# Holding the expert part of an attention and mixture-of-experts kernel to its source order

## The chip, the cores and the metric

The kernel runs on one NeuronCore of a Trainium2 chip. The metric is the device time of one execution in microseconds; for each kernel the median of its runs is given. TensorE (PE in the profile), VectorE (DVE), ScalarE (ACT), GpSimd (POOL) and SyncE (SP) each take their own list of instructions and wait for each other by semaphores.

## The reference, cut to what matters

```python
# block-sparse attention: batch 4, 8 heads, 768 positions, width 64
scores = q @ k.T / 8                      # masked by blocks of 32
attn = softmax(where(mask, scores, -1e9))
x = (attn @ v) laid out as 3072 tokens x 512
# experts: 8, hidden width 1024
P = balance(exp(x @ w_gate))              # 8 rounds of row and column scaling
for e in range(8):
    out += P[:, e:e+1] * (maximum(x @ w1[e], 0) @ w2[e])
```

## The kernel before, in words

The attention part comes first. Its work is put into numbered time slots by hand (the table `plan_at`), and the loop at L888 to L890 issues it slot by slot. `in_order` (L878) ties each instruction that a step issues to the newest one on the same engine, so that every engine takes the attention part's instructions in the order in which the loop issues them. The tie is a dependency without a semaphore, `behind` (L873).

The expert part follows in the source. It is cut into 32 iterations `i`: expert `e = i // 4` on a quarter of the tokens `b = i % 4`. Each iteration has two stages.

`stage1(i, qi)` (L1126), one of four quarters of the first matrix product, is a Strassen-like scheme: seven products `p0, p1, p5, p6, p3, p4, p2` in this order, each of six matmuls of 384 columns (L1135), since every operand is split into a high and a low 16-bit part and three of the four combinations are taken, for two halves of the inner dimension. A product's high weights feed the first two matmuls and the low weights the third. VectorE combines the products as they come (`comb`, L1145) into `r11`, `a1`, `u3`, `c21`; ScalarE copies the first product out of PSUM (L1180), applies the relu (L1184, L1200, L1204, L1212) and writes the high part of each result `h` (L1155); the low part is made by VectorE (L1159, L1165) or by GpSimd (L1165). GpSimd also forms four sums of the results (L1207, L1033). Four PSUM buffers `ph` hold products, so the fifth product of a row needs the first one's buffer back.

`stage2(i, p)` (L1233) takes the seven products of the second matrix, each in three pieces of twelve matmuls of 256 columns (L1248), and VectorE adds each piece into the output accumulator (L1269). Four other PSUM buffers, `py`, hold the pieces. In the main loop the pieces of iteration `i` stand between the quarters of iteration `i + 1`: p0, p1, quarter 0, p5, quarter 1, p6, p3, quarter 2, p4, p2, quarter 3.

Beside this regular work there is work per expert: the loads of `w1` and `w2` (L173, through one staging tile `r`), eight reductions for the scale of each (L187), the sums of weight quadrants on GpSimd (L1026) and the splits of the seven weight pieces into a high part on ScalarE (L1011) and a low part on VectorE (L1015). The first products of the next expert are in the last iteration of this one (`b == 3`): there, `w1` is split into the single buffers `arena` and `attic` that hold the seven pieces.

Which of this is written where is decided by the class `Slots` (L940). It counts ticks, one for each product or piece; it charges costs to three engines and issues queued work when it is due and fits. `need` (L993) issues what a coming product requires at once, just ahead of that product (L1131, L1236 to L1240). The order in which the source issues is thus a plan. But the program is built with `schedule_with_timeline_sim=True` (L1385), and in the expert part nothing ties the instructions to that plan: the scheduler lines each engine's instructions up by its own simulation, under the true dependencies alone. It also moves instructions of the expert part in among the last of the attention part, and the attention's leftovers (`finish_x`, L348) ahead of where the source has them. `PIN` is 0, so `InOrder` (L893) passes calls through.

Of the kernel before, what the change touches and what calls it, by code (L numbers as in the profile page):

```python
# [55 lines left out]
def tile_sparse_attention_moe(  # L56
# [11 lines left out]
    nc = tc.nc  # L68
# [156 lines left out]
    def load_x1(i, p):  # L225
        nc.sync.dma_start(out=xp[p], in_=xd[i % B][:, p])
# [168 lines left out]
    with ExitStack() as actx:  # L395
# [479 lines left out]
        )  # L875
        newest = {}

        def in_order(fn, *a):  # L878
            n = len(nc.cur_bb.bb.instructions)
            fn(*a)  # L880
            for ins in nc.cur_bb.bb.instructions[n:]:
                if ins.engine in newest:
                    tc.add_manual_dep(
                        ins, newest[ins.engine], behind, reason="keep_in_program_order"
                    )
                newest[ins.engine] = ins.name

        for T in range(min(plan_at), max(plan_at) + 1):  # L888
            for _, _, fn, a in sorted(plan_at.get(T, ()), key=lambda x: x[:2]):
                in_order(fn, *a)  # L890
        xlast = finish_x(B - 1)

    class InOrder:  # L893
        def __init__(self, engine):
# [226 lines left out]
    def load_x(i):  # L1121
        b = i % B
        for p in PORDER:
            load_x1(i, p)
# [183 lines left out]
    for i in range(NI):  # L1308
# [48 lines left out]
        quarter(3)  # L1357
        if i + 2 < NI:
            load_x(i + 2)

# [27 lines left out]
```

## Time and profile before

| | before |
|---|---|
| median of 3 runs | 2358.24 us (2353.56 to 2359.13) |
| profiled execution, own time | 2357.4 us |
| its span | 2355.6 us |
| mean granted TensorE clock | 0.986 |
| busy: PE, DVE, ACT, POOL | 2200.1, 2014.4, 1256.0, 1287.1 us |

The page of the profile gives for each engine the time in which it worked and, for each group of instructions, the idle time ahead of them and who ended it. The chain of waits follows the last instruction back to what released it. The view by windows gives the busy time of every engine in chosen stretches, with the granted clock of TensorE; the view in order of time gives single instructions, with start and duration, where instructions alike that follow each other are one row. Time in rows is counted from the start of the span. An iteration's place is found by counting the matmuls of L1135 and L1248.

### The profile page before, as it was taken

How to read it: one execution, taken by the hardware profiler on the slowest of the kernel's cores; microseconds unless marked ns; L12 is line 12 of the kernel's file. 1: busy time of each engine (PE TensorE's matmuls, PEld its weight loads, DVE VectorE, ACT ScalarE, POOL GpSimd, SP SyncE). 2: the span in 40 equal slices, each digit the busy share in tenths (PEclk: the TensorE clock that was granted, in tenths of full speed). 3: DMA queues.
4: the chain of work that ended last, by engine and by line, in shares of the span. 5: the costliest groups of instructions: out<-in, count | busy, mean ns of one | idle time of the engine just before them, and what ended most of it. 6: DMA issues, size and time to landing. Idle time of an engine off the chain costs nothing.

```text
span 2355.6 us, 47334 instructions
## 1 busy us (share of the span) xinstructions
PE 2200.1 (93%) x18892; PEld 1608.6 (68%) x18892; DVE 2014.4 (86%) x3570; ACT 1256.0 (53%) x2173; POOL 1287.1 (55%) x1235
## 2 busy tenths in 40 slices
PE   5999998879999999999989999999899999998999
PEld 3766666647666677677667776776677667766777
DVE  8999999888789878987898789878987898789876
ACT  4888878655465445444444445444544454445442
POOL 2012334496367645765576557655865486548543
PEclk9999999999999999999999999999999999999999
DMA  6667765422121212121212121212211221121221
GB/s 152 135 123 151 186 131 121 135 97 75 48 82 50 83 48 83 48 83 48 83 48 83 48 84 52 80 48 83 64 68 48 84 80 52 48 84 48 75 75 54
DMA packets 191888, 192.34 MB, mean 82 GB/s; under 512 B 131740, under 2 KB 144052, under 8 KB 191668
## 3 DMA queue, kind: packets, MB, share of 16 engines
q1 hardware_dynamic: 191104, 189.30, 28.2%
q8 instruction: 147, 2.41, 0.4%
q14 instruction: 73, 0.60, 0.1%
q10 hardware_dynamic: 564, 0.03, 0.0%
HBM read 140.54 MB, written 17.30 MB: 67 GB/s over the span
## 4 chain that ended last, share of the span: by engine, by line
PE 57%; DVE 21%; POOL 9%; issue 6%; DMA 4%; ACT 3%; SPq 0%; DVEq 0%; POOLq 0%; ACTq 0%
PE py L1248 25%; PE p L1135 23%; POOL r L1026 3%; DVE top L673 3%; DMA r<-in_moe_w_dram 3%; DVE h L1165 2%; PE u L731 2%; POOL h L1165 2%; DVE u L1145 2%; DVE acc L1269 2%; DVE mx_w L187 2%; PE t L697 1%; PE m L664 1%; PE t L700 1%; PE m L667 1%
## 5 line engine op out<-in xcount | busy, mean ns | idle before, releaser
L1248 PE MATMUL py<-w2p,h 128*128 128x256 f16 x8064 | 971.1, 275 | 52.7 <-ACT h L1155 23.7
L1248 PEld LDWEIGHTS <-h 128*128 128x128 f16 x8064 | 790.1, 99 | 209.9 <-ACT h L1155 28.8
L1269 DVE SCALAR_TENSOR_TENSOR acc<-py,spare,acc 128x256 f32<-128x256 f32 (+1 forms) x840 | 459.2, 581 | 49.5 <-PE py L1248 46.9
L1165 POOL TENSOR_TENSOR h<-u,h 128x384 f16<-128x384 f32 x128 | 127.0, 992 | 601.3 <-ACT h L1155 601.3
L1135 PEld LDWEIGHTS <-attic 128*128 128x128 f16 x3072 | 301.8, 98 | 195.9 <-issue 22.5
L1135 PE MATMUL p<-attic 128*128 128x384 f16 x2304 | 413.2, 328 | 16.4 <-DVE r L1145 14.4
L1135 PE MATMUL p<-arena 128*128 128x384 f16 x2304 | 407.6, 327 | 19.4 <-DVE a L1145 11.2
L1135 PEld LDWEIGHTS <-arena 128*128 128x128 f16 x2304 | 225.9, 98 | 153.5 <-issue 24.8
L1155 ACT ACTIVATE h<-c 128x384 f16<-128x384 f32 x256 | 133.6, 522 | 330.7 <-DVE c L1145 256.7
L705 ACT ACTIVATE pe<-t,shift,qk 128x768 int32<-128x768 f32 x192 | 189.7, 989 | 78.6 <-PE t L700 73.0
L1145 DVE SCALAR_TENSOR_TENSOR a<-p,a 128x384 f32<-128x384 f32 x384 | 211.1, 550 | 18.9 <-PE p L1135 14.3
L673 DVE TENSOR_REDUCE top<-m 128x1 f32<-128x768 f32 x192 | 181.8, 949 | 16.7 <-PE m L667 16.4
L1155 ACT ACTIVATE h<-r 128x384 f16<-128x384 f32 x256 | 132.5, 521 | 66.5 <-POOL r L1033 63.0
L1207 POOL TENSOR_TENSOR s<-a,u 128x384 f32<-128x384 f32 x128 | 129.6, 1013 | 68.7 <-ACT a L1204 68.7
L1033 POOL TENSOR_TENSOR r<-s,r 128x384 f32<-128x384 f32 x128 | 155.4, 1214 | 9.6
L1033 POOL TENSOR_TENSOR c<-c,r 128x384 f32<-128x384 f32 x128 | 150.8, 1178 | 10.0
L1135 PE MATMUL p<-arena,attic 128*128 128x384 f16 x768 | 146.1, 327 | 0.0
L1026 POOL TENSOR_TENSOR r<-r 128x256 f32<-128x256 f32 (+1 forms) x106 | 135.0, 1290 | 20.0 <-DVE arena L1015 17.9
L664 PE MATMUL m<-kt,qt 128*128 128x512 f16 (+1 forms) x384 | 129.6, 338 | 14.5 <-DVE top L673 7.2
L1165 POOL TENSOR_TENSOR h<-r,h 128x384 f16<-128x384 f32 x128 | 142.8, 1115 | 0.2 <-ACT h L1155 0.2
L1145 DVE SCALAR_TENSOR_TENSOR r<-p,a 128x384 f32<-128x384 f32 x128 | 70.7, 552 | 79.0 <-PE p L1135 59.4
L697 PE MATMUL t<-qt,kt 128*128 128x512 f16 (+1 forms) x384 | 127.9, 333 | 10.8 <-DVE top L673 10.6
(206 smaller groups left out, 3683.1 us busy)
## 6 DMA issues: line engine op xcount, KB each, us to landing
arena<-xd SPq DMA_DIRECT2D x128, 384.0 KB, 3.9
attic<-xd SPq DMA_DIRECT2D x96, 384.0 KB, 3.9
r<-in_moe_w_dram SPq DMA_DIRECT2D x16, 2048.0 KB, 8.4
arena<-in_q_dram SPq DMA_DIRECT2D x16, 384.0 KB, 4.5
arena<-in_k_dram SPq DMA_DIRECT2D x16, 384.0 KB, 4.8
arena<-in_v_dram SPq DMA_DIRECT2D x4, 1536.0 KB, 8.5
xd<-xs_t SPq DMA_DIRECT2D x16, 384.0 KB, 4.6
out_dram<-acc SPq DMA_DIRECT2D x24, 256.0 KB, 2.0
```

Source lines behind the costliest of these rows:

```text
L664: nc.tensor.matmul(sc[:, lo:hi], lhsT=qt[:, 0, c], rhs=ka[:, lo:hi], start=True, stop=False)
L673: nc.vector.tensor_reduce(out=tops[n][:, c : c + 1], in_=sc[:, :S], axis=AX.X, op=ALU.max)
L697: nc.tensor.matmul(sc[:, lo:hi], lhsT=kt[:, 0, c], rhs=qa[:, lo:hi], start=True, stop=False)
L705: nc.scalar.activation(pe, sc[:, :S], AF.Exp, bias=shift, scale=qk[n // 2][3])
L1026: lambda c=c: Pinned.gpsimd.tensor_tensor(out=out[:, c], in0=x[:, c], in1=y[:, c], op=op),
L1033: nc.gpsimd.tensor_tensor(out=out, in0=x, in1=y, op=ALU.subtract)
L1135: nc.tensor.matmul(ps, lhsT=w1p[p][:, l, kc, fs], rhs=xp[p][:, r, kc], start=(kc == 0 and m == 0), stop=(kc == KH - 1 and m == 2),)
L1145: nc.vector.scalar_tensor_tensor(out=t, in0=ps, scalar=HDOWN, in1=other, op0=ALU.mult, op1=ALU.add)
L1155: nc.scalar.activation(h[:, 0], src, AF.Relu if relu else AF.Copy)
L1165: eng.tensor_tensor(out=h[:, 1], in0=src, in1=h[:, 0], op=ALU.subtract)
L1248: nc.tensor.matmul(py, lhsT=hs[i, p, kc][:, l, tsl], rhs=w2p[p][:, r, kc], start=(kc == 0 and m == 0), stop=(kc == KF // 2 - 1 and m == 2),)
L1269: nc.vector.scalar_tensor_tensor(out=dst, in0=src, scalar=c, in1=dst, op0=ALU.mult, op1=ALU.add)
```

## The change

The list of traced instructions is kept, the tie is put into a function of its own, `hold_from(n)`, and the length of the list at the end of the attention part is remembered. At the end of the kernel every instruction issued since then is tied to the newest before it on its engine. No instruction is added or taken away, no operand or size differs. Lines after L890 stand six further down.

```diff
+        traced = nc.cur_bb.bb.instructions
+
+        def hold_from(n):
+            for ins in traced[n:]:
                 if ins.engine in newest:
                     tc.add_manual_dep(
                         ins, newest[ins.engine], behind, reason="keep_in_program_order"
                     )
                 newest[ins.engine] = ins.name
 
+        def in_order(fn, *a):
+            n = len(traced)
+            fn(*a)
+            hold_from(n)
+
         for T in range(min(plan_at), max(plan_at) + 1):
...
         xlast = finish_x(B - 1)
+        held = len(traced)
...
         if i + 2 < NI:
             load_x(i + 2)
+    hold_from(held)
```

What this does to the engines' lists is shown at three places. In the names, `p5_12_0` is product p5 of iteration 12, quarter 0, and the last number of a name only tells tiles apart.

**VectorE where the first products of expert 3 begin** (iteration 12, quarter 0, with stage 2 of iteration 11 around it). L1015 (after: L1021) are the low parts of the `w1` splits: a split that reads `s3` is that of product 6. Before:

```order
L1015 SCALAR_TENSOR_TENSOR attic_96<-s3_3_14764,sw1_3_14762,attic_96 128x1024
L1145 SCALAR_TENSOR_TENSOR u3_11_3_16024<-p6_11_3_16025,a1_11_3_15995 128x384
L1165 TENSOR_TENSOR h_5_8094<-r11_11_3_16004,h_5_8094 128x384
L1015 SCALAR_TENSOR_TENSOR attic_96<-r1_3_14758,sw1_3_14762,attic_96 128x1024
L1145 SCALAR_TENSOR_TENSOR c21_11_3_16033<-p3_11_3_16034,u3_11_3_16024 128x384
L1015 SCALAR_TENSOR_TENSOR arena_92<-r1_3_14758,sw1_3_14762,arena_92 128x1024
L1015 SCALAR_TENSOR_TENSOR attic_96<-r1_3_14758,sw1_3_14762,attic_96 128x1024
L1145 SCALAR_TENSOR_TENSOR u3_11_3_16024<-p4_11_3_16044,u3_11_3_16024 128x384
L1145 SCALAR_TENSOR_TENSOR a1_11_3_15995<-p4_11_3_16044,a1_11_3_15995 128x384
L1015 SCALAR_TENSOR_TENSOR attic_96<-r1_3_14758,sw1_3_14762,attic_96 128x1024
```

Now:

```order
L1021 SCALAR_TENSOR_TENSOR arena_92<-r1_3_14758,sw1_3_14762,arena_92 128x1024
L1151 SCALAR_TENSOR_TENSOR r11_12_0_16193<-p1_12_0_16194,a1_12_0_16184 128x384
L1171 TENSOR_TENSOR h_0_8089<-r11_12_0_16193,h_0_8089 128x384
L1151 SCALAR_TENSOR_TENSOR a1_12_0_16184<-p5_12_0_16205,a1_12_0_16184 128x384
L1021 SCALAR_TENSOR_TENSOR attic_96<-s3_3_14764,sw1_3_14762,attic_96 128x1024
L1151 SCALAR_TENSOR_TENSOR u3_12_0_16215<-p6_12_0_16216,a1_12_0_16184 128x384
L1021 SCALAR_TENSOR_TENSOR attic_96<-r1_3_14758,sw1_3_14762,attic_96 128x1024
L1151 SCALAR_TENSOR_TENSOR c21_12_0_16224<-p3_12_0_16226,u3_12_0_16215 128x384
L1021 SCALAR_TENSOR_TENSOR attic_96<-r1_3_14758,sw1_3_14762,attic_96 128x1024
L1151 SCALAR_TENSOR_TENSOR u3_12_0_16215<-p4_12_0_16237,u3_12_0_16215 128x384
L1151 SCALAR_TENSOR_TENSOR a1_12_0_16184<-p4_12_0_16237,a1_12_0_16184 128x384
L1021 SCALAR_TENSOR_TENSOR attic_96<-r1_3_14758,sw1_3_14762,attic_96 128x1024
```

The splits stood among the combinations of the last quarter of iteration 11; now those of products 6, 3, 4 and 2 stand one by one between the combinations of iteration 12's first quarter, each behind the combination of the product just ahead of it.

**ScalarE where iteration 13 begins.** `w2p_5` and so on are the high parts of the `w2` splits, `a1_13_0` the copy of the first product out of PSUM, `h` from `s1`, `a1`, `r11`, `c21` the high parts of the sums that GpSimd makes. Before:

```order
L1155 ACTIVATE h_23_8112<-u3_12_3_16734 128x384
L1212 ACTIVATE c21_12_3_16744<-c21_12_3_16744 128x384
L1204 ACTIVATE a1_12_3_16700<-a1_12_3_16700 128x384
L1011 ACTIVATE w2p_5_8087<-t2_3_16273,sw2_3_16271 128x1024
L1011 ACTIVATE w2p_6_8088<-r2_3_16267,sw2_3_16271 128x1024
L1180 ACTIVATE a1_13_0_16894<-p0_13_0_16895 128x384
L1011 ACTIVATE w2p_3_8085<-r2_3_16267,sw2_3_16271 128x1024
```

Now:

```order
L1161 ACTIVATE h_24_8113<-s1_12_3_16778 128x384
L1161 ACTIVATE h_25_8114<-a1_12_3_16700 128x384
L1161 ACTIVATE h_26_8115<-r11_12_3_16710 128x384
L1161 ACTIVATE h_27_8116<-c21_12_3_16744 128x384
L1017 ACTIVATE w2p_5_8087<-t2_3_16273,sw2_3_16271 128x1024
L1017 ACTIVATE w2p_6_8088<-r2_3_16267,sw2_3_16271 128x1024
L1017 ACTIVATE w2p_3_8085<-r2_3_16267,sw2_3_16271 128x1024
L1017 ACTIVATE w2p_4_8086<-r2_3_16267,sw2_3_16271 128x1024
L1186 ACTIVATE a1_13_0_16894<-p0_13_0_16895 128x384
```

The copy stood behind two splits; now four high parts that wait for GpSimd and four splits stand ahead of it.

**SyncE's loads around the first loads for expert 4.** `xd` are the stored tokens of a quarter, `r1` and `r2` the weights. Before:

```order
L173 DMA r2_3_16267<-in_moe_w2_dram 128x8x512
L226 DMA arena_92<-xd_1_77 128x1536 x4
L226 DMA attic_96<-xd_1_77 128x1536 x3
L173 DMA r1_4_17448<-in_moe_w1_dram 128x4x1024
L226 DMA arena_92<-xd_2_78 128x1536 x4
L226 DMA attic_96<-xd_2_78 128x1536 x3
```

Now:

```order
L173 DMA r2_3_16267<-in_moe_w2_dram 128x8x512
L226 DMA arena_92<-xd_1_77 128x1536 x4
L226 DMA attic_96<-xd_1_77 128x1536 x3
L226 DMA arena_92<-xd_2_78 128x1536 x4
L226 DMA attic_96<-xd_2_78 128x1536 x3
L173 DMA r1_4_17448<-in_moe_w1_dram 128x4x1024
```

The load of the next `w1` now stands behind seven token loads, the last of which waits for the end of iteration 13's first stage.

4 lines of the change are left out of this document (removed).

## The prediction

> **What bounds the kernel now.** I read the page first, then the chain of waits, the windows and single instructions in order of time. The page:
>
> ```profile
> span 2355.6 us, 47334 instructions
> PE 2200.1 (93%) x18892; PEld 1608.6 (68%) x18892; DVE 2014.4 (86%) x3570; ACT 1256.0 (53%) x2173; POOL 1287.1 (55%) x1235
> PE 57%; DVE 21%; POOL 9%; issue 6%; DMA 4%; ACT 3%; SPq 0%; DVEq 0%; POOLq 0%; ACTq 0%
> ```
>
> TensorE is the largest share of the chain. The chain in order of time gives its pace and the rhythm of the experts:
>
> ```profile
> 805.34 3.90 PE p L1135 x24
> 812.71 7.32 PE py L1248 x67
> ...
> 931.79 8.52 DMA r<-in_moe_w_dram
> ...
> 2101.10 8.50 DMA r<-in_moe_w_dram
> ```
>
> A matmul of stage 1 takes 3.90/24 = 0.1625 us, one of stage 2 7.32/67 = 0.109 us. An expert has 672 of the one and 1008 of the other: 109.2 + 110.1 = 219.3 us. The same load recurs after five experts: (2101.10 - 931.79)/5 = 233.9 us. So TensorE loses 14.6 us per expert. Three windows show where: the last iteration of one expert (11), the first of the next (12), and an ordinary one (columns: busy time of PE, weight loads, DVE, ACT, POOL, each with its count, granted clock, DMA).
>
> ```profile
> 1152.00:1214.00 62.00, 57.18 (x431) 41.57 (x429) 57.96 (x99) 31.63 (x57) 35.22 (x31) 1.00 0.27 86
> 1214.00:1270.00 56.00, 50.27 (x371) 36.23 (x369) 52.17 (x81) 25.36 (x48) 46.61 (x44) 0.97 0.23 78
> 1277.00:1328.00 51.00, 51.00 (x397) 38.78 (x396) 40.74 (x78) 23.59 (x47) 27.02 (x28) 1.00 0.14 48
> ```
>
> Ordinary iterations have no idle TensorE at all; nothing can be gained there. All that an order can win back is the 14.6 us at seven expert changes, about 102 us, and the start. VectorE is nearly full at the change (57.96 of 62), so where it stands waiting there is what matters.
>
> **The change part by part.** No work is added. Each term is a wait that an ordered engine meets.
>
> Durations, from the groups by form and single instructions in order of time:
>
> ```profile
> L1207 POOL TENSOR_TENSOR s<-a,u 128x384 f32<-128x384 f32 x128 | 129.6, 1013 | 68.7 <-ACT a L1204 68.7
> L1033 POOL TENSOR_TENSOR r<-s,r 128x384 f32<-128x384 f32 x128 | 155.4, 1214 | 9.6
> L1165 POOL TENSOR_TENSOR h<-r,h 128x384 f16<-128x384 f32 x128 | 142.8, 1115 | 0.2 <-ACT h L1155 0.2
> L1026 POOL TENSOR_TENSOR r<-r 128x512 f32<-128x512 f32 x42 | 68.5, 1651 | 17.9 <-DVE arena L1015 17.9
> L1026 POOL TENSOR_TENSOR r<-r 128x256 f32<-128x256 f32 x64 | 66.5, 1053 | 2.2 <-DVE w2p L1015 2.2
> L1011 ACT ACTIVATE w2p<-r,sw 128x1024 f16<-128x1024 f32 x48 | 53.9, 1141 | 59.8 <-POOL r L1026 54.4 <-DVE sw L204 5.4
> ...
> L1180 ACT ACTIVATE a<-p 128x384 f32<-128x384 f32 x128 | 61.5, 481 | 57.5 <-PE p L1135 56.2 <-POOL s L1026 0.2
> ...
> L1015 DVE SCALAR_TENSOR_TENSOR w2p<-r,sw,w2p 128x1024 f16<-128x1024 f32 x48 | 78.3, 1634 | 12.0 <-ACT w2p L1011 12.0
> ```
> ```profile
> 1162.39 1.27 DVE L1015 SCALAR_TENSOR_TENSOR attic<-r,sw,attic 128x1024 f16<-128x1024 f32 x1
> 1290.34 0.56 DVE L1145 SCALAR_TENSOR_TENSOR r<-p,a 128x384 f32<-128x384 f32 x1 [1.54 <-PE p L1135]
> 1292.04 0.56 DVE L1165 TENSOR_TENSOR h<-r,h 128x384 f16<-128x384 f32 x1 [0.24 <-ACT h L1155]
> ```
> ```profile
> 1290.93 0.52 ACT L1184 ACTIVATE r<-r 128x384 f32<-128x384 f32 x1 [1.15 <-DVE r L1145]
> 1291.48 0.52 ACT L1155 ACTIVATE h<-r 128x384 f16<-128x384 f32 x1
> ```
>
> *First quarter of a new expert.* Zero is where stage 2 of iteration 11 starts. TensorE needs 72 x 0.109 = 7.9 us for p0 and p1, then seven products of 0.975 us: the quarter would end at 14.7. Product 5 needs a split of a quadrant that GpSimd subtracts after the first split has read it. GpSimd, in order, still has the previous quarter (its first low part, then s, a, r, c, five at 1.0 to 1.2, from about 1.8 to 7.2), then half a sum (1.65), two low parts (2.1), the other half (1.65): 12.6. ScalarE's high part takes it to 13.7, VectorE's low part to 15.0; the two first matmuls need only the high part, the other four and their drain take 0.8: product 5 is there at 15.8 instead of 10.8. From here the rows of VectorE above run one after the other. ScalarE copies product 0 behind the split of product 6 (13.7 + 1.14 + 0.48 = 15.3); `r11` starts, its low part 1.70 later (1292.04 - 1290.34), `a1` at 17.5, the split for product 6 until 19.2, product 6 at 20.0; then `u3` 0.55, the next split 1.2, product 0.8: 22.6; then `c21` 0.55, ScalarE's high part 0.52, its split 1.14, VectorE's 1.2, product 0.8: 26.9; then `u3`, the relu and high part of it, both splits, the last product: 0.5 + 1.1 + 1.14 + 1.2 + 0.7 = 4.7: 31.6. The quarter ends 16.9 us late. Before, the splits ran ahead, with the first product's stall of 1.66 us and one of 1.38 us the only ones around it:
>
> ```profile
> 1164.65 1.14 PE L1135 MATMUL p<-arena 128*128 128x384 f16 x6 [1.66 <-DVE a L1145]
> 1167.16 4.26 PE L1248 MATMUL py<-w2p,h 128*128 128x256 f16 x34 [1.38 <-DVE acc L1269]
> ```
>
> Bounds: 12 us, if half of the sums' part is already over when the stretch begins, to 19 with the splits at the 1.63 us that they average under GpSimd's traffic.
>
> *Start of the next iteration.* The 15 sums for `w2` that stand before GpSimd's part of the last quarter take 15 x 1.05 = 15.8 us, with two low parts 18; TensorE gives that part some 9.5 us to wait in, of which about 1.5 is spent: `s`, `a`, `r`, `c` come about 6.5 us late. ScalarE now waits for all four, then has four splits (4 x 1.14), and only then copies the first product: 7.2 + 6.5 + 4.6 = 18.3 us after the quarter's end, while TensorE fills its four PSUM buffers by 7.9 + 3.9 = 11.8. That is 6.5 us, and VectorE's queued splits and the scale of `w2` add some 4.5: I take 11. Before, the same trap shut once here, ScalarE waiting for GpSimd and TensorE for ScalarE:
>
> ```profile
> 1233.38 1.15 ACT L1011 ACTIVATE w2p<-r,sw 128x1024 f16<-128x1024 f32 x1 [3.72 <-POOL r L1026]
> ```
> ```profile
> 1237.93 3.53 PE L1248 MATMUL py<-w2p,h 128*128 128x256 f16 x17 [3.21 <-ACT h L1155]
> ```
> ```profile
> 1234.00:1242.00 8.00, 4.77 (x27) 2.86 (x26) 7.33 (x9) 3.34 (x7) 6.41 (x6) 0.79 0.53 183
> ```
>
> Bounds: 5.7 (the idle time of the second window above, 56 - 50.27) to 16.
>
> These rows also show a price behind a wait: 17 matmuls took 3.53 us where 17 x 0.109 = 1.9 would do, with a granted clock of 0.79. The stalls of the first quarter are shorter, and the 1.66 and 1.38 us above left the clock at 1.00. I put nothing for it in the sum, and 1.6 us for each change in the upper end. [...]
>
> *The load of w1.* It waited only for its staging tile before, was issued in iteration 12 and its maxima ran at once:
>
> ```profile
> 1236.49 0.38 SPq L173 DMA_DIRECT2D r<-in_moe_w_dram  x1
> ```
> ```profile
> 1175.17 1.87 DVE L187 TENSOR_REDUCE mx_w<-r 128x1 f32<-128x512 f32 x3 [2.27 <-DMA r<-in_moe_w_dram]
> 1247.67 4.82 DVE L187 TENSOR_REDUCE mx_w<-r 128x1 f32<-128x512 f32 x8
> ```
> ```profile
> 1165.81 0.38 SPq L173 DMA_DIRECT2D r<-in_moe_w_dram  x1
> ```
>
> Such a load took 1175.17 - 1165.81 = 9.4 us. Now it goes out about 1 us into iteration 13, behind the token loads, and lands at 10.4 or later; VectorE comes to the first maximum at 8.5 to 9 and stands there, the next quarter's combinations behind it. With two PSUM buffers of slack I take 3 us; bounds 0 and 5. In return the 4.82 us of maxima leave the crowded iteration 12; that is in the 11 above.
>
> A change of experts then costs 16.9 + 11 + 3 = 30.9 us instead of 14.6: 16.3 more, seven times, 114 us.
>
> *Ordinary quarters.* VectorE now waits for the low part of `r11` before the next combination (1.14 us idle, 1290.90 to 1292.04). A quarter behind six pieces absorbs it in its PSUM buffers. The quarter behind three pieces only (p5) finds the copy of its first product behind high part `r` on ScalarE: by the rows above its sixth buffer is about 0.3 us late. 31 times 0.35 is 11 us; bounds 0 and 30.
>
> *Start.* Before, stage 1 began at 462.2:
>
> ```profile
> L1135 PE MATMUL p<-arena x2304: 322/326/524, 462.2 to 2320.3; 128*128 128x384 f16 x192
> ...
> 462.00:560.00 98.00, 84.25 (x668) 58.02 (x666) 82.33 (x136) 54.45 (x105) 76.48 (x69) 0.96 0.16 59
> ```
>
> Now it begins behind the last transposes of the attention, which follow the normalisation of the last head and the scale of `w2`: about 468, 5.7 later. Four quarters then run without pieces between them, each bound by the loop TensorE, VectorE, ScalarE, GpSimd, and `finish_x` makes TensorE wait in the open; but before, the 98 us also held 13.75 idle. I take 12 us in all; bounds 0 and 25.
>
> The sum: 2357.4 + 114 + 11 + 12 = 2494 us. The profiled execution is 0.8 us under the median, which changes nothing: I say 2494.
>
> **The rivals.**
> 1. *The plan smooths the expert change.* For it: VectorE's 4.82 us of maxima and GpSimd's sums for `w1` leave the busiest iteration, and the plan spreads the rest by due times. If the splits were ready one product ahead, the idle time of the first window (62 - 57.18 = 4.8 us) would go and about a third of the second one's 5.7, 6.7 us at each change, and with the start unchanged that gives 2357.4 - 7 x 6.7 = 2310 us. It decides in the first quarter: below about 5 us lost there the change gains. Against it: the order puts four splits behind combinations that need the very product before, so they can't be ahead. Chance 0.06.
> 2. *Only the first quarter pays.* The stops let the others catch up, so that 16.9 replaces all of the 14.6 and nothing follows it: 2357.4 + 7 x 2.3 + 11 + 12 = 2396 us. For it: VectorE was full before, and a stop of TensorE frees it. Chance 0.14.
> 3. *The waits reach ordinary quarters.* For it: VectorE has 40.74 busy of 51 there, and two waits of about 1 us in each of four quarters take 8 of the 10 that are left. If a third of them comes through, 0.7 us a quarter, 31 x 4 x 0.7 = 87 us come on top: 2581 us. Against it: PSUM buffers carry it over. Chance 0.14.
> 4. *The order changes nothing that counts* (within 0.3%, about what a measurement of this kernel can tell from no change): 0.02. That the ties do not hold is ruled out by the engines' lists.
>
> **How the numbers follow.** My forecast has 0.64. Its own bounds are 7 x (12 + 5.7 + 0 - 14.6) = 22 and 7 x (19 + 16 + 5 + 1.6 - 14.6) = 189, with 0 to 55 for the rest; not all ends meet, so it goes from 2410 to 2580. The range of 2396 to 2585 takes in rivals 2 and 3 and leaves out 1 and the ends of the others. Slower: 0.64 + 0.14 + 0.14 = 0.92; same 0.02; faster 0.06.
>
> **What would show it.** Right: the first products of experts 1 to 7 stand four matmuls at a time, 2 to 4 us apart, with TensorE idle behind VectorE's splits; ScalarE stands before its first `w2` split of an iteration after an expert change and TensorE behind the copy; the load of experts recurs after about 250 us; ordinary windows stay full. Wrong: a period under 234 us, or idle time of TensorE in the windows of ordinary iterations of more than 1 us each.

## The result, and the profile after

The tied kernel takes 2606.55 us (median of 4 runs, 2603.8 to 2616.57) beside 2357.37 us of the kernel before: a ratio of 1.1067, 95% interval 1.1034 to 1.1101. The order costs 249 us; the prediction said 2494 us, 137 more than before, and at most 2585.

The profiled execution took 2616.57 us. Its first matmul of stage 1 came at 470.2 us; in the other profiled runs, whose attention part is the same, it lies anywhere from 456.5 to 470.4. So the stages are counted here from that matmul. The page, to set beside the three lines of before:

```profile
span 2614.6 us, 47460 instructions
...
PE 2284.1 (87%) x18892; PEld 1627.5 (62%) x18892; DVE 1998.0 (76%) x3570; ACT 1270.0 (49%) x2173; POOL 1248.8 (48%) x1235
...
PE 44%; DVE 27%; POOL 10%; ACT 8%; issue 7%; DMA 4%; SPq 0%; DVEq 0%; POOLq 0%
```

TensorE's share of the chain fell from 57 to 44%, VectorE's rose from 21 to 27%. And 18892 matmuls, the same as before, are busy for 2284.1 us instead of 2200.1: the same work takes 84 us more inside the matmuls. The windows show where (columns: busy time of PE, weight loads, DVE, ACT, POOL with counts, granted clock, DMA): the first quarter of expert 3; the first of the next iteration; the one in which `w1` lands; an ordinary iteration but for its last quarter; and the stretch with the four quarters of iteration 0, which begin at 470.2.

```profile
1272.90:1301.80 28.90, 13.48 (x45) 4.38 (x43) 15.43 (x19) 9.85 (x13) 9.48 (x8) 0.60 0.00 1
1355.00:1370.70 15.70, 9.72 (x44) 4.99 (x43) 12.17 (x16) 9.34 (x13) 7.21 (x7) 0.78 0.00 0
1420.50:1431.50 11.00, 8.21 (x45) 4.50 (x44) 7.94 (x16) 1.81 (x4) 1.78 (x2) 0.87 0.16 67
1474.70:1523.70 49.00, 48.26 (x380) 37.08 (x379) 37.03 (x68) 21.82 (x45) 26.88 (x27) 1.00 0.08 27
462.00:510.00 48.00, 38.07 (x242) 22.71 (x240) 29.85 (x54) 21.85 (x43) 22.59 (x23) 0.82 0.15 49
```

A quarter is 42 matmuls of 0.1625 us, 6.83 us at full pace. The first takes 28.9 us and no engine is busy for much more than half of it: they wait for each other. TensorE's instructions there in order of time, with the idle time ahead of each and who ended it:

```profile
1275.12 0.50 PE L1141 MATMUL p<-arena 128*128 128x384 f16 x2 [1.08 <-ACT arena L1017]
1277.09 0.82 PE L1141 MATMUL p<-arena 128*128 128x384 f16 x4 [1.47 <-DVE arena L1021]
1280.26 0.82 PE L1141 MATMUL p<-arena 128*128 128x384 f16 x2 [2.35 <-ACT arena L1017]
1282.61 1.46 PE L1141 MATMUL p<-arena 128*128 128x384 f16 x4 [1.53 <-DVE arena L1021]
...
1299.04 0.82 PE L1141 MATMUL p<-attic 128*128 128x384 f16 x2 [2.80 <-ACT attic L1017]
1300.36 1.46 PE L1141 MATMUL p<-attic 128*128 128x384 f16 x4 [0.50 <-DVE attic L1021]
1301.61 4.59 PE L1254 MATMUL py<-w2p,h 128*128 128x256 f16 x22
```

Two matmuls behind ScalarE's high part, four behind VectorE's low part, product after product: the predicted rhythm. Not predicted is that the same four matmuls take 0.82 us at 1277.09 and 1.46 at 1282.61, and 22 of stage 2 then 4.59 where 22 x 0.109 = 2.4 would do.

The other two foreseen places are there as well. ScalarE waits for GpSimd's sums ahead of splits of `w2`, copies the first product only behind them, and TensorE, with its four buffers full, waits for that copy:

```profile
1362.47 2.19 ACT L1017 ACTIVATE w2p<-r,sw 128x1024 f16<-128x1024 f32 x2 [1.12 <-POOL r L1032]
1364.57 0.47 ACT L1186 ACTIVATE a<-p 128x384 f32<-128x384 f32 x1
```
```profile
1365.09 5.78 PE L1141 MATMUL p<-attic 128*128 128x384 f16 x18 [5.98 <-ACT a L1186]
```

The load of `w1` is issued, takes 10.5 us to land, and VectorE's first maxima wait for it:

```profile
1413.27 0.38 SPq L173 DMA_DIRECT2D r<-in_moe_w_dram  x1
...
1423.73 3.06 DVE L187 TENSOR_REDUCE mx_w<-r 128x1 f32<-128x512 f32 x5 [1.92 <-DMA r<-in_moe_w_dram]
```

In iteration 0, TensorE waits for the first `w2` split, which ScalarE has behind the quarters, and for the attention's leftovers on VectorE:

```profile
519.82 0.37 PE L1254 MATMUL py<-w2p,h 128*128 128x256 f16 x1 [5.89 <-ACT w2p L1017]
577.96 0.19 PE L369 MATMUL lg<-gh,xs_b 128*128 128x8 f16 x1 [5.80 <-DVE xs_b L355]
```

Counting matmuls gives each iteration's length, from the end of its predecessor's stage 2 to the end of its own. Means over experts 1 to 6, in us; full pace is 219.3/4 = 54.8. "Start" runs from the first matmul of stage 1 to the end of stage 2 of iteration 2.

| kernel | b = 3 | b = 0 | b = 1 | b = 2 | sum | first quarter | start | over before, same chip |
|---|---|---|---|---|---|---|---|---|
| before | 60.2 | 64.0 | 54.9 | 54.8 | 233.9 | mixed | 218.3 | |
| all tied | 80.4 | 67.2 | 62.1 | 55.8 | 265.4 | 28.9 | 255.6 | 249.2 |
| e1 start only | 60.4 | 64.0 | 54.9 | 54.8 | 234.2 | mixed | 253.3 | 41.5 |
| e2 changes only | 80.0 | 67.2 | 62.0 | 55.9 | 265.0 | 28.9 | 226.0 | 214.3 |
| e3 filler | 77.5 | 67.2 | 62.0 | 55.8 | 262.5 | 26.9 | 255.2 | 234.6 |
| e4 early splits | 71.3 | 66.3 | 61.8 | 55.8 | 255.1 | 7.1 | 255.3 | 179.6 |
| e5 staggered | 71.9 | 66.1 | 61.8 | 55.8 | 255.6 | 8.8 | 255.2 | 181.7 |
| e6 late maxima | 80.0 | 67.2 | 59.9 | 55.8 | 263.0 | 28.9 | 253.1 | 235.1 |
| e7 costs | 77.8 | 74.8 | 61.9 | 55.8 | 270.3 | 28.9 | 259.8 | 293.6 |
| e9 TensorE only | 70.0 | 64.9 | 54.9 | 54.8 | 244.6 | 12.9 | 225.8 | 71.6 |
| e10 all but TensorE | 79.5 | 66.9 | 59.7 | 54.2 | 260.3 | 34.3 | 250.7 | 212.5 |
| e11 VectorE only | 70.1 | 66.5 | 57.0 | 53.8 | 247.5 | 28.0 | 273.6 | 144.0 |
| e12 all but VectorE | 80.4 | 63.6 | 60.6 | 54.9 | 259.5 | 26.0 | 224.2 | 178.8 |
| e13 VectorE, ScalarE free | 74.3 | 61.3 | 59.3 | 54.8 | 249.7 | 20.5 | 218.3 | 111.7 |
| e14 ScalarE only | 40.8 | 96.0 | 60.8 | 54.8 | 252.5 | 30.8 | 232.9 | 140.6 |

So 37 us of the 249 arise in the start (255.6 - 218.3), the rest behind it, nearly all at the expert changes and the loads of `w1`. "Mixed" means that pieces of stage 2 stand inside the quarter; that is so in e10, e11 and e14 too, so their quarters can't be set beside the others. The last column is the difference of the medians. Each experiment has two runs (e15 seven); the 95% interval of such a difference is 7 to 9 us either way, and 12 to 13 for e1 and e18.

### The profile page after: what moved, and what is told of

It reads as the page before. It is cut to its first block, busy times and chain, and to the rows that moved or that the text cites. A ratio compares the mean times of both kernels' runs of the same rounds, so it can differ in the third digit from the quotient of the medians.

```text
span 2614.6 us, 47460 instructions
## 1 busy us (share of the span) xinstructions
PE 2284.1 (87%) x18892; PEld 1627.5 (62%) x18892; DVE 1998.0 (76%) x3570; ACT 1270.0 (49%) x2173; POOL 1248.8 (48%) x1235
## 4 chain that ended last, share of the span: by engine, by line
PE 44%; DVE 27%; POOL 10%; ACT 8%; issue 7%; DMA 4%; SPq 0%; DVEq 0%; POOLq 0%
PE py L1254 19%; PE p L1141 17%; ACT h L1161 3%; DVE acc L1275 3%; DMA r<-in_moe_w_dram 3%; POOL r L1032 3%; DVE h L1171 3%; DVE top L673 3%; DVE u L1151 2%; POOL h L1171 2%; DVE a L1151 2%; DVE mx_w L187 2%; PE u L731 2%; POOL s L1213 1%; DVE attic L1021 1%
## 5 line engine op out<-in xcount | busy, mean ns | idle before, releaser
L1254 PE MATMUL py<-w2p,h 128*128 128x256 f16 x8064 | 923.9, 276 | 14.8 <-ACT w2p L1017 6.8
L1254 PEld LDWEIGHTS <-h 128*128 128x128 f16 x8064 | 799.5, 99 | 134.7 <-issue 14.8
L1141 PE MATMUL p<-attic 128*128 128x384 f16 x2304 | 456.6, 349 | 152.9 <-DVE a L1151 46.0
L1275 DVE SCALAR_TENSOR_TENSOR acc<-py,spare,acc 128x256 f32<-128x256 f32 (+1 forms) x840 | 449.6, 581 | 37.9 <-PE py L1254 26.6
L673 DVE TENSOR_REDUCE top<-m 128x1 f32<-128x768 f32 x192 | 181.9, 950 | 18.7 <-PE m L667 18.3
L1171 DVE TENSOR_TENSOR h<-r,h 128x384 f16<-128x384 f32 x128 | 89.4, 699 | 134.4 <-ACT h L1161 134.2
L1161 ACT ACTIVATE h<-r 128x384 f16<-128x384 f32 x256 | 133.9, 523 | 81.8 <-POOL r L1039 77.8
L1171 DVE TENSOR_TENSOR h<-s,h 128x384 f16<-128x384 f32 x128 | 111.1, 868 | 79.5 <-ACT h L1161 78.7
L1141 PE MATMUL p<-arena,attic 128*128 128x384 f16 x768 | 154.6, 338 | 12.1 <-DVE attic L1021 12.1
L1190 ACT ACTIVATE r<-r 128x384 f32<-128x384 f32 x128 | 66.9, 523 | 183.0 <-DVE r L1151 183.0
L1039 POOL TENSOR_TENSOR r<-s,r 128x384 f32<-128x384 f32 x128 | 145.8, 1139 | 10.0
L664 PE MATMUL m<-kt,qt 128*128 128x512 f16 (+1 forms) x384 | 130.0, 339 | 14.6 <-DVE top L673 7.2
L1206 ACT ACTIVATE u<-u 128x384 f32<-128x384 f32 x128 | 66.9, 523 | 150.1 <-DVE u L1151 148.0
```

Source lines behind the costliest of these rows:

```text
L664: nc.tensor.matmul(sc[:, lo:hi], lhsT=qt[:, 0, c], rhs=ka[:, lo:hi], start=True, stop=False)
L673: nc.vector.tensor_reduce(out=tops[n][:, c : c + 1], in_=sc[:, :S], axis=AX.X, op=ALU.max)
L1039: nc.gpsimd.tensor_tensor(out=out, in0=x, in1=y, op=ALU.subtract)
L1141: nc.tensor.matmul(ps, lhsT=w1p[p][:, l, kc, fs], rhs=xp[p][:, r, kc], start=(kc == 0 and m == 0), stop=(kc == KH - 1 and m == 2),)
L1161: nc.scalar.activation(h[:, 0], src, AF.Relu if relu else AF.Copy)
L1171: eng.tensor_tensor(out=h[:, 1], in0=src, in1=h[:, 0], op=ALU.subtract)
```

## The experiments

In what follows "over before" is the last column of the table, and each text in front of a result is what was expected of it. Theory at the outset: the predicted waits are the right ones, and TensorE's clock, which falls behind them (0.60 over the first quarter, in the windows above), makes them longer. Rivals: steady losses in ordinary quarters, the start, one engine's order alone, or plain lack of VectorE's time.

**Where it is lost.** In e1 the tie ends at iteration 2, as the diff shows, and in e8 at iteration 1; in e2 it begins at iteration 2 (`held = len(traced)` there); in e16 it holds for two of four iterations.

```diff
         if i == 2:
             finish_late()
+            hold_from(held)
...
-    hold_from(held)
```

> Only the instructions from the end of the attention part to the beginning of iteration 2 are tied; the rest is lined up by the scheduler as before. Theory (the traces put some 45 us of the 249 into the start and the rest into the seven expert changes): 2357 + 45 = 2402 us, 2385 to 2415. Rival (the start costs what the prediction gave it, 12 us, and the waits of the changes are spread wider than they look): 2369 us, 2360 to 2380.

It took 2397.65 us, 41.5 over before, as the theory had it. The prediction's 12 us is ruled out: the interval of the ratio begins at 1.0117, which is 28 us.

> Only the instructions from iteration 2 on are tied. Theory: 2357 + 7 x 30 = 2570 us, 2550 to 2590, with the same waits at the changes as in the changed kernel. Rival (the late start of the changed kernel puts its later order out of step and causes part of these waits): under 2530 us.

It took 2570.38 us, 214.3 over before, as the theory had it. Together, 41.5 + 214.3 = 255.8 us come near the 249 of the tied kernel: start and changes are nearly independent.

> Tied only from the end of the attention part to the beginning of iteration 1: the first iteration's quarters, the products of iteration 0 with the quarters of iteration 1 between them, not the balance rounds' second half and the attention's leftovers in iteration 1. Theory (about half of the start's 41 us is lost there, by quarters that run without pieces between them, the rest in iteration 1 by the leftovers and the balance): 2357 + 20 = 2377 us, 2368 to 2385. Rival (one of the halves holds it all): 2357 to 2362 us, or 2393 to 2400 us.

It took 2392.74 us, 34.1 over before, at the edge of what the rival said: tying no more than the first iteration costs most of the start's 41.5, and by their intervals the two can't be told apart. What the free scheduler wins back in iteration 1 it loses in the next, and by stage 2's end of iteration 2 the start is 245.6 long, beside 253.3 in e1 and 218.3 before. TensorE waits 11.64 us in the open for the attention's leftovers:

```profile
582.27 0.19 PE L369 MATMUL lg<-gh,xs_b 128*128 128x8 f16 x1 [11.64 <-DVE xs_b L355]
```

For e16, the iterations with b = 1 and 2 are tied one by one from expert 1 on (`if i > 2 and b in (1, 2): hold_from(held)`, `held` renewed in each).

> Tied are only the instructions that iterations b = 1 and b = 2 of each expert issue, the load of w1, its maxima and the ordinary quarters among them; the changes of experts proper and the start are free. Theory: the step of b = 1 rises from 54.9 to about 62 us, that of b = 2 from 54.8 to 55.8 us, eight experts at the most: 2358 + 55 to 65 = 2413 to 2423 us. Rival (the wait for w1 follows from the late iteration 12 of the tied order and goes without it): 2358 to 2385 us.

It took 2407.9 us, 50.8 over before: 5 us under the theory's range, but much nearer to it than to the rival's. The lengths of its iterations are 59.7 (b = 1) and 55.8 (b = 2), and the free ones beside them lose too (62.8 and 64.6). An ordinary iteration loses 1.0 us, the load of `w1` about 4.8; the rest of the 7.3 in the tied kernel must come with its surroundings, which are tied there too.

**The clock.** e3 gives TensorE something to do in the waits:

```diff
+            if i and i % B == 0 and qi == 0 and p in (6, 3, 4, 2):
+                for _ in range(9):
+                    nc.tensor.matmul(
+                        ps, lhsT=w1p[0][:, 0, 0, fs], rhs=xp[0][:, 0, 0],
+                        start=True, stop=True,
+                    )
             for kc in range(KH):
```

> The changed kernel with nine more matmuls of 384 columns ahead of products 6, 3, 4 and 2 of the first quarter of each new expert, on operands that are there already, into the product's own PSUM buffer, which the product then starts afresh: 4 x 9 x 0.1625 = 5.9 us of work for TensorE in waits of about 3.8 us each. Theory (the low clock behind waits is a cost of its own): the granted clock of that quarter rises from 0.60 to 0.8 or more, its groups of four matmuls take 0.65 to 0.9 us instead of 1.46, the 22 matmuls behind it 2.4 to 3.2 instead of 4.59, and seven changes gain 4 to 6 us each: 2565 to 2580 us. Rival (the four matmuls are slow for another reason, or the clock doesn't follow the busy share): 1.46 us as before and 2606 us or up to 40 us more.

It took 2590.71 us, 234.6 over before: 14.6 less than the tied kernel, a third to a half of what the theory gave. Its rows show the mechanism (single instructions, the first ahead of the filler, the others behind it; the page; the window of the quarter):

```profile
1270.38 1.46 PE L1147 MATMUL p<-arena 128*128 128x384 f16 x4 [1.53 <-DVE arena L1021]
...
1286.57 0.82 PE L1147 MATMUL p<-attic 128*128 128x384 f16 x4 [0.82 <-DVE attic L1021]
1287.23 4.09 PE L1260 MATMUL py<-w2p,h 128*128 128x256 f16 x36
```
```profile
PE 2292.7 (89%) x19144; PEld 1643.5 (64%) x19144; DVE 1998.7 (77%) x3570; ACT 1270.7 (49%) x2173; POOL 1248.6 (48%) x1235
```
```profile
1260.60:1287.30 26.70, 16.44 (x82) 7.63 (x80) 15.49 (x19) 9.86 (x13) 9.55 (x8) 0.87 0.00 1
```

With filler, four matmuls take 0.82 us again and 36 of stage 2 take 4.09, with the granted clock at 1.00 from 1287.30 to 1291.20; over the quarter it is 0.87 instead of 0.60. But the quarter is still 26.7 us long: the clock of this quarter is some 2 to 3 us of each change (14.6/7; 80.4 to 77.5), the chain of engines the rest. It may be a little more, since two of the four fillers had no wait left behind them and so stood in the way themselves.

**The splits of `w1`.** e4 issues the first four among the combinations of the quarter ahead of the change, the other three around stage 2's first products:

```diff
         comb(a1, product(5), a1)
+        if split:
+            split(0)
...
         if last:
-            split_w1(e + 1)
+            after[i](4)
         stage2(i, 0)
+        if last:
+            after[i](5)
         stage2(i, 1)
```

> The changed kernel, all tied, but the source issues the splits of w1 earlier: the first four among the combinations of the last quarter ahead of the change, the other three around stage 2's first two products. Theory (these splits between the combinations are what stretches the first quarter to 28.9 us): that quarter falls to 8 to 12 us, at full clock, VectorE's queue gives 2 to 4 us back in the quarter before, and seven changes gain 13 to 20 us each: 2470 to 2515 us. Rival (VectorE and GpSimd are full there, so the wait only moves into stage 2 or the quarter before): over 2560 us.

It took 2535.72 us, 179.6 over before: between the two. The quarter fell from 28.9 to 7.1 us, at a granted clock of 0.97. But the iteration fell from 80.4 to 71.3 only; over half of the gain went into waits earlier in it, in stage 2:

```profile
1248.08 0.40 PE L1279 MATMUL py<-w2p,h 128*128 128x256 f16 x1 [6.15 <-DVE h L1182]
1252.72 5.30 PE L1279 MATMUL py<-w2p,h 128*128 128x256 f16 x24 [4.25 <-DVE acc L1300]
```

e5 takes the waits out of that chain: each low part stands one product behind its high part, and product 6 is split ahead of product 5. Two of its lines beside those of e4:

```diff
-            lambda: one(5, a[0, 0]),
-            lambda: one(6, s3),
...
+            lambda: (low(1), sums((a[0, 1], a[0, 1], a[0, 0], 2)), high(6)),
+            lambda: (low(6), high(5)),
```

> As the early splits, but VectorE's low part of a split stands one product behind ScalarE's high part, product 6 is split ahead of product 5, and the last low part is left to the first quarter. Theory (with the early splits, 10 us went into stage 2 because VectorE stood 1.6 to 1.9 us before each split for ScalarE, and ScalarE for VectorE): those stops go, the step of the iteration with the splits falls from 71.6 to 60 to 64 us, and seven changes gain 8 to 11 us each over 2536 us: 2460 to 2480 us. Rival (VectorE has too much work there, about 11 us of splits in two quarters, in whatever order): within 15 us of 2536 us.

It took 2540.35 us, 181.7 over before, as the rival had it. VectorE no longer stands in the stretch with the splits, and that wins nothing, since it is full there (third busy column, 21.00 of 21.00), and TensorE waits for its additions:

```profile
1237.60:1258.60 21.00, 16.63 (x112) 11.81 (x111) 21.00 (x24) 11.05 (x16) 16.28 (x11) 0.84 0.25 92
```
```profile
1249.09 5.13 PE L1291 MATMUL py<-w2p,h 128*128 128x256 f16 x24 [4.37 <-DVE acc L1312]
```

> The kernel before, nothing tied in the expert part, with the source of the staggered splits. Theory (untied, the scheduler moves the splits to where it wants them, whatever the source says): within 1 per cent of 2358 us, 2335 to 2382. Rival (it takes the source's order wherever its simulation sees no difference, and the splits now come before combinations that TensorE needs): over 2382 us, or, if the staggered place is the better one, under 2335 us.

The same source with nothing tied took 2363.15 us, a ratio to before of 1.0025 (1.0012 to 1.0038), as the theory had it: a source order that moves the tied kernel by 66 us moves the free one by 6.

**The plan's due times and costs.**

> The changed kernel with the eight maxima of w1 due ten ticks later in the plan, so that VectorE meets them about one quarter later. Theory (VectorE stands before the first maximum until w1 has landed, and TensorE behind it, with a low clock after it: some 6 to 7 us a change): the step of that iteration falls from 62.0 to 56 to 58 us, seven times: 2562 to 2580 us. Rival (the iteration is long because the 8 maxima are extra work for VectorE): the wait moves into the next quarter, within 10 us of 2606 us.

(`6 if k == 0` becomes 16 for `w1`.) It took 2593.77 us, 235.1 over before, some 14 less than the tied kernel: this misses both. The first quarter of that iteration falls to 7.0 us, but now a later product waits, and TensorE stands ahead of the small transpose that spreads the scale:

```profile
1422.79 2.11 PE L1141 MATMUL p<-attic 128*128 128x384 f16 x12 [1.32 <-DVE r L1151]
...
1435.98 0.32 PE L110 MATMUL all_w<-ident,ma_w 128*128 128x128 f32 x1 [2.22 <-DVE ma_w L193]
```

> The changed kernel, all tied, with the plan's costs set to durations of the trace: a sum of weights on GpSimd 1.05 or 1.65 us instead of 0.6 or 1.2, its low part 1.1 instead of 0.9, its sums of a quarter 4.7 instead of 3.9, a split 1.14 on ScalarE and 1.6 on VectorE instead of 1.04 and 1.2. The plan then puts 4 of the 15 sums for w2 ahead of the last quarter's part on GpSimd, and the copy of the next first product ahead of four splits of w2. Theory (the wait of 5.98 us at the start of the next iteration, and the slow matmuls behind it, come from that order): that step falls from 67.0 to 57 to 61 us; the splits of w1 and the start stay as they were: 2606 - 7 x 8 = 2550 us, 2535 to 2570. Rival (the splits of w2 have to be made anyway and only move to the next quarters): over 2585 us.

It took 2652.29 us, 293.6 over before. That is in the rival's range and by its mechanism, but neither side expected it to be slower than the tied kernel, by some 45 us. The copy does come ahead of the splits and the quarter at 15.7 us falls to 7.0; but the splits of `w2` are now late for stage 2, which needs them in the same iteration (b = 0 takes 74.8 us instead of 67.2):

```profile
1364.95 5.50 PE L1254 MATMUL py<-w2p,h 128*128 128x256 f16 x35 [4.78 <-DVE w2p L1021]
```

> The changed kernel, all tied; the small transposes that spread the scale of w1 and of w2 over the partitions (13 waits, 20.2 us in the changed kernel, none before) come six ticks behind VectorE's last maximum instead of two. Theory (TensorE reaches a transpose whose operand VectorE has not made, and the products behind it wait): 12 to 25 us less, 2582 to 2595 us. Rival (VectorE is behind there with everything, so the next combination holds TensorE instead): over 2600 us.

(`gap=2` at `spread` becomes 6.) It took 2607.99 us, 251.5 over before, as the rival had it. TensorE's waits, with total, count and longest, in the tied kernel and then in e17:

```profile
PE p L1141 <- ACT a L1186: 39.5, 14, 6.0
...
PE all_w L110 <- DVE ma_w L193: 20.2, 13, 2.3
PE p L1141 <- DVE r L1151: 16.0, 9, 3.1
```
```profile
PE p L1141 <- ACT a L1186: 52.5, 22, 7.0
...
PE p L1141 <- DVE r L1151: 23.1, 17, 3.1
```

The 20.2 us are gone, and two rows have grown by 13.0 and 7.1: the wait has moved on.

> All tied, with three edits of the source together: the staggered splits, the later maxima of w1, the later transposes. Theory (their waits stand at different places and add): 2606 - 66 - 13 - 15 = 2512 us, 2495 to 2520. Rival (they share VectorE's backlog, so that one gives back what another wins): over 2528 us.

It took 2480.95 us, 124.5 over before: better than the sum of the three. Alone they win some 66, 13 and nothing, together 126 us; which of them makes another worth more was not tried in pairs. Of what is left, some 35 us are the start, 253.0 long here, which the three hardly shorten. At the changes TensorE's largest wait is for VectorE's additions (total, count, longest):

```profile
PE py L1291 <- DVE acc L1312: 72.7, 30, 5.3
```

**Whose order.** In e9 to e14 `hold_from(held, tied)` skips the instructions of engines that stay free:

```diff
             for ins in traced[n:]:
+                if not tied(ins.engine):
+                    continue
```

> Only TensorE is tied to the source order; VectorE, ScalarE, GpSimd and SyncE are lined up by the scheduler around it. Theory (VectorE's splits between the combinations hold up everybody; free VectorE can make them ahead, so TensorE's order waits for little): under 60 us of the 249, below 2417 us. Rival (TensorE's own order is what costs: before, it drew pieces of stage 2 in between products 5, 6 and 3 of the first quarter, and tied it can only stand): over 125 us, above 2482 us.

It took 2431.56 us, 71.6 over before: between the two. VectorE makes the splits early, and TensorE has one long wait in the quarter, 4.88 us.

> All engines but TensorE are tied. Theory: over 150 us of the 249 stay, above 2507 us, since TensorE can draw ahead only what VectorE has delivered the operands for. Rival (TensorE's order): under 125 us, below 2482 us, with pieces of stage 2 drawn into the waits of the first quarter.

It took 2572.38 us, 212.5 over before, as the theory had it. TensorE does draw pieces of stage 2 into the quarter, and then runs dry against the same splits:

```profile
1276.36 0.82 PE L1143 MATMUL p<-attic 128*128 128x384 f16 x2 [2.25 <-ACT attic L1019]
```

> Only VectorE is tied. Theory: over 125 us, above 2482 us, with the splits between the combinations of the first quarter as in the changed kernel. Rival (TensorE's order, or the waits of ScalarE and GpSimd on each other): under 60 us, below 2417 us.

It took 2503.91 us, 144.0 over before, as the theory had it; 55 of them are the start (273.6 - 218.3).

> All engines but VectorE are tied. Theory: under 125 us stay, below 2482 us: the four waits behind splits in the first quarter shrink, while ScalarE's copy behind four splits of w2 and the start remain. Rival (TensorE's order, or ScalarE's and GpSimd's): over 190 us, above 2547 us.

It took 2538.72 us, 178.8 over before: the theory said less than 125 at the changes and the start together, so it falls; the rival's 190 is not reached either. The start is nearly cured (224.2), the first quarter is not (26.0):

```profile
1239.93 0.82 PE L1143 MATMUL p<-attic 128*128 128x384 f16 x2 [2.25 <-ACT attic L1019]
```

With VectorE free, TensorE waits for ScalarE's high part: ScalarE's list has each split behind the relu and high part of the product before. So the chain of split, product and combination seems to hang in both lists. That is the theory's second form, which the next two runs test.

> Only ScalarE is tied. Theory, second form: the chain is there again, 60 to 130 us over the 2360 us, 2420 to 2490 us, with a first quarter of over 22 us, and the start, which is VectorE's, within 10 us of before. Rival (ScalarE is only half busy and waits off the path): under 2400 us.

It took 2497.7 us, 140.6 over before: more than that form gave (60 to 130 us, with 10 of them in the start, where 14.6 are), and far from the rival's 2400. TensorE runs ahead with stage 2 (b = 3 is done in 40.8) and pays in the next iteration (96.0), where `w2`'s splits are late:

```profile
PE py L1256 <- ACT w2p L1019: 62.5, 18, 7.8
```

> TensorE, GpSimd and SyncE are tied, VectorE and ScalarE are not. Theory, second form (the source order of VectorE and that of ScalarE each hold the same chain of splits and combinations, so that freeing one leaves it and freeing both takes it away): 2430 to 2465 us, near the 2432 us with TensorE alone tied, and the first quarter at 13 to 16 us instead of 26 to 29. Rival (GpSimd's sums, or TensorE's inability to draw pieces ahead, keep the chain): over 2500 us.

It took 2468.86 us, 111.7 over before: between, 4 us above the theory's range, and the quarter takes 20.5 us instead of 13 to 16. One wait of 9 us is left in the quarter, that of product 5, seven times. GpSimd's tied list has the sum for it behind a quarter's four sums and two low parts, just as counted in the prediction:

```profile
1210.31 0.82 PE L1143 MATMUL p<-arena 128*128 128x384 f16 x2 [9.17 <-ACT arena L1019]
```
```profile
1204.55 1.57 POOL L1034 TENSOR_TENSOR r<-r 128x512 f32<-128x512 f32 x1
1206.08 0.90 POOL L1173 TENSOR_TENSOR h<-r,h 128x384 f16<-128x384 f32 x1
1206.95 0.90 POOL L1173 TENSOR_TENSOR h<-c,h 128x384 f16<-128x384 f32 x1
1207.82 3.70 POOL L1034 TENSOR_TENSOR r<-r 128x512 f32<-128x512 f32 x3
```

Tying one engine after another gives 71.6 (TensorE), 111.7 (and GpSimd, SyncE), 178.8 (and ScalarE), 249.2 (and VectorE). Alone, TensorE, VectorE and ScalarE cost 71.6 + 144.0 + 140.6 = 356 us, more than all together, so the costs overlap: the same chain stands in several lists, and freeing one list leaves most of it (212.5 us without TensorE's order, 178.8 without VectorE's). The orders of GpSimd and of SyncE were not tried alone.

## Why the prediction was wrong

The direction and each named place were right: four matmuls at a time in the first quarter, ScalarE's copy behind the splits of `w2`, VectorE ahead of `w1`, full ordinary windows; the load of experts recurs after 265 us, for the "about 250". What failed is the size of the terms, by three steps: each chain was priced with mean durations, or with rows from quieter places, and nothing was put in the sum for the work right behind a wait; a row of short waits was taken to leave TensorE's clock alone, which fell to 0.50; and at the start the idle time of before was counted as room. Every term was too small for one change or iteration, only the start of the next iteration within its bounds. In us for one change, over full pace:

| term, as the prediction put it | predicted | measured |
|---|---|---|
| first quarter | 16.9 | 28.9 - 6.8 = 22.1 |
| rest of that iteration | 0 | 80.4 - 54.8 - 22.1 = 3.5 |
| start of the next iteration | 11 | 67.2 - 54.8 = 12.4 |
| load of `w1` | 3 | 62.1 - 54.8 = 7.3 |
| ordinary, each iteration | 0.35 | 55.8 - 54.8 = 1.0 |
| start, once | 12 | 37.3 in the trace, 41.5 timed (e1) |

Seven changes at 38.0 in place of 7 x 14.6, six loads of `w1` at 7.3, some nine ordinary iterations at 1 and the start make 7 x 23.4 + 44 + 9 + 37 = 254 us; the measured 249 us have their places. Of the 117 us between this sum and the prediction's 137, the first quarter has 7 x 5.2 = 36, the start 25, the rest of the iteration 7 x 3.5 = 25, the load of `w1` 23 and the start of the next iteration 10; the ordinary iterations have 2 less than was put for them.

*First quarter, bounds 12 to 19: too short by 5.* The chain was counted to end 31.6 us after stage 2 began (1265.0); it ended at 36.8. Of these 5.2 us, 3.3 were there at product 5, predicted for 15.8 and finished at 1282.61 + 1.46, that is 19.1. GpSimd ended its part 1.4 us later than counted, since its sums and low parts took up to 1.89 us instead of 1.0 to 1.2 (its halves of a quadrant's sum were shorter than counted, 1.28 instead of 1.65); the split of product 5 took 2.31 us instead of 1.27; and the four matmuls behind it ran at a granted clock of 0.50, in 1.46 us instead of 0.82:

```profile
1280.23 2.31 DVE L1021 SCALAR_TENSOR_TENSOR arena<-r,sw,arena 128x1024 f16<-128x1024 f32 x1 [2.81 <-ACT arena L1017]
```

```profile
1271.60 1.86 POOL L1039 TENSOR_TENSOR c<-c,r 128x384 f32<-128x384 f32 x1
...
1275.91 1.89 POOL L1171 TENSOR_TENSOR h<-c,h 128x384 f16<-128x384 f32 x1
```

The prediction had the 1.63 average of the splits in its upper end only, and 1.0 to 1.2 for each of these. The other 1.9 us are about what e3 gains in this quarter with the clock brought back from 0.60 to 0.87 (28.9 to 26.9 us).

*Clock, 0 in the sum, 1.6 in the upper end.* This step failed as reasoning. The prediction took two waits of 1.66 and 1.38 us that had left the clock at 1.00 as a licence for a row of such waits. The tied kernel's windows in that quarter:

```profile
1275.00:1277.50 2.50, 0.91 (x5) 0.40 (x6) 2.42 (x3) 0.06 (x1) 2.50 (x2) 1.00 0.03 7
1277.50:1280.20 2.70, 0.41 (x3) 0.02 (x1) 0.00 (x0) 1.15 (x2) 2.70 (x3) 0.67 0.00 0
1280.20:1284.10 3.90, 2.32 (x7) 0.86 (x8) 2.78 (x2) 2.43 (x5) 1.27 (x2) 0.50 0.00 0
...
1288.00:1301.00 13.00, 5.74 (x17) 1.44 (x16) 5.84 (x7) 3.65 (x5) 0.91 (x1) 0.50 0.00 0
```

The clock falls behind idle times of 1.08 and 1.47 us and early in the one of 2.35, and then stays at 0.50: if it goes from 1.00 to 0.50 at once, 0.67 over the second window puts the fall at 1278.4. From 1275.0 to there TensorE had worked for 0.91 + 0.41 = 1.32 us, and the longest idle time of the quarter so far was 1.47. Behind the longer stop there is a slow stretch as well: the 18 matmuls behind 5.98 us took 5.78 us instead of 2.9, at a granted clock of 0.52. On the time, e3, whose fillers stand behind product 5, puts the low clock of that quarter at 14.6 us in all, or a little more. The 84 us of longer matmuls are thus not 84 us of time. In e3 the matmuls of stage 1, its 252 fillers left out, are busy for 961.5 us instead of 987.1 and those of stage 2 for 915.8 instead of 923.9, together 34 us less than in the tied kernel, and the kernel wins 14.6: more than half of that time stood where there would have been a wait anyway. What the clock cost behind the other two waits (0.78 and 0.87 in their windows) was not measured by itself.

*Rest of the iteration and start of the next.* 12.4 instead of 11 is within its bounds, and the trap is the predicted one: the copy was done 17.9 us after the quarter's end (18.3 predicted), and TensorE stood 5.98 us (6.5). But the size is partly luck. The 6.5 us by which GpSimd's sums come late do not follow from the 18, 9.5 and 1.5 that they are drawn from: these give 10, or 7 with the 1.5 counted as room. In the trace the 15 sums took 12.0 us instead of 15.8 and the last of the four came 11.5 us after the quarter's end instead of 13.7, while the four splits lost 1.1 in a wait of their own. The 4.5 us put for VectorE's queue came from no row; 6.4 are there, 2.9 of them the slow 18 matmuls. For the rest of the change's own iteration nothing had been put: the matmuls right behind the first quarter run on at a granted clock of 0.55 (22 in 4.59 us instead of 2.4, above), and its third quarter takes 8.9 us instead of 6.8, with a wait for the transpose of `w2`'s scale.

*Load of w1, bounds 0 to 5: 7.3.* The landing was nearly right, 11.0 us behind the first product of iteration 13's stage 2 (1412.7), for "10.4 or later". What was missing is what comes behind: VectorE's 1.92 us become waits of 1.76 and 1.03 for TensorE, and 36 matmuls at a granted clock of 0.67, 6.10 us instead of 36 x 0.109 = 3.9:

```profile
1427.31 1.14 PE L1141 MATMUL p<-attic 128*128 128x384 f16 x6 [1.76 <-DVE r L1151]
1429.48 2.08 PE L1141 MATMUL p<-attic 128*128 128x384 f16 x6 [1.03 <-DVE a L1151]
1431.36 6.10 PE L1254 MATMUL py<-w2p,h 128*128 128x256 f16 x36
```

*Start, bounds 0 to 25: short by 25 to 29 us, the largest miss of a single place.* The prediction took the 13.75 idle us of before as room to pay from, and added quarters that would run without pieces. The tied VectorE keeps neither: its order alone brings 55 us (e11), without it 6 are left (e12). Which of VectorE's steps there weighs most wasn't tried apart.

*Rivals.* The third, losses in ordinary quarters, gave 2581 us, the nearest to the result, but for the wrong reason: those lose 1.0 us an iteration, where it had 2.8. The second, that only the first quarter pays, falls with the 12.4 and 7.3 us behind it. The first, that the plan smooths the change, falls with the first quarter; the best tied order tried is still 124.5 us over the free one (e18).

## What to carry to other kernels

When an order is fixed across several in-order engines, write down for each moved step which lists hold it: a chain that stands in two or three lists is not cured by freeing one, and removing a single wait moves it to the next late operand (e6, e7, e17). A row of waits is not the sum of its single waits; price it with the slow durations that the trace shows in crowded places, and ask what a half-busy TensorE does to its clock (here it was busy for 13.48 of 28.90 us and the clock was 0.60). A plan that looks right by its own costs needs a look at which engine is full there: VectorE was at the change, and no source order tried here could hide that.

## What was not expected of the hardware

In the tied kernel the granted clock went from 1.00 to 0.50 behind two idle times of 1.08 and 1.47 us, half a microsecond into a third; over the whole quarter TensorE was busy 47% of the time (13.48 of 28.90). In e3 matmuls ran without a stop from 1270.38; the clock was 0.50 from 1270.4 to 1272.4, 0.56 from there to 1274.2 and 1.00 behind it, so that, if it rose at once, it was back at 1274.0, 3.6 us into them.

Where the clock is read in ever narrower windows, it is at 0.50 in the tied kernel from 1278.43 to 1305.74, from 1363.76 to 1370.59 and from 1428.62 to 1435.44, and in the kernel before from 1237.42 to 1240.83: 27.31, 6.83, 6.83 and 3.41 us. These lengths are whole multiples of 3.41 us, as is that of every other slow stretch in these two traces which the end of the run does not cut off, and the shortest is 3.41. In the kernel before, the matmuls of stage 2 were dense again from 1237.93, and the clock was still at 0.50 until 1240.83.

VectorE's 128 x 1024 split took 1.93 and 2.31 us where GpSimd was at work beside it, and 1.27 to 1.29 us in the four later splits of the same quarter, where GpSimd stood. No run here tells whether that is the cause.
